# Another order of the start: the first rows of w3 by columns, products of zeros in front, banks emptied by ScalarE, one turning a step

## The chip, the cores and the metric

The kernel runs on one core of a Trainium2 chip. The metric is the device time of the launch in microseconds (us); lower is better. Before the change it is 537.89 us, the median of three runs from 537.82 to 539.18.

## The reference

Attention over a local window and a few global positions, with a bias that grows with distance, and then a feed-forward layer with a gate:

```python
# batch 4, heads 8, sequence 768, head size 64; n_global 8, n_local 96
scores = scale * np.matmul(q, k.transpose(0, 1, 3, 2))
keep = is_global | is_local                 # local: 0 <= rel < n_local
dist = np.where(is_global & ~is_local, float(n_local), np.abs(rel))
scores = np.where(keep, scores - slopes * dist, -1e9)
a = softmax(scores)                         # rows, with 1e-9 added to the sum
x = np.matmul(a, v)                         # as (3072 tokens, 512)
# feed-forward: w1, w2 (512, 1024), w3 (1024, 1024), w_out (1024, 512)
out = ((x @ w1) * (x @ w2)) @ w3 @ w_out
```

The weights arrive as 64-bit floats, two 32-bit words to a number. `n_global` and `n_local` arrive as 64-bit integers.

## The kernel before

As `w3 @ w_out` doesn't depend on the tokens, the kernel folds the two into one matrix of 1024 x 512 (eight row blocks f of 128 rows) at the start. A fold of one row block is eight products in full fp32 over the column blocks k (`F.f.k`, line 171, two records each in the trace), one PSUM bank to a block. The product is then split in a high part (`ph`, ScalarE, L174, rounds to fp32r) and a low part (`pl`, VectorE, L177). w1 and w2 are split in the same way (`wh`, L161, and `wl`, L165), one pair of 128 columns (W0 to W7) at a time. Every product with the weights is then three products in fp32r: high by high, low by high, high by low (L196 to L198 with w1 and w2, called `U`, and L224 to L226 with the folded matrix, called `Z`).

The 64-bit words are put into 32 bits by three integer operations on VectorE, `A`, `B` and `C` (L150, L152, L154). Pieces are called by kind: `o0` to `o3` are one row block of w_out each (512 KB in DRAM), `O2` and `O3` two each; `t10` is the first half of w3's row block 1 (512 KB) and `t11` the second, `T4` a whole one (1 MB). They are fetched (`d.`, L124, all on SP's queue) into eight half slots, each free again when its piece's C is done. The converted blocks of w3 lie in a pool of three buffers (tag `ag`), which later holds the gate products.

Attention runs in 24 steps s of 128 queries, for all heads: `S` scores on TensorE (L505), `R` the bias, maxima and copy on VectorE (L514, for q in 0 to 3, two operations each), `E` exponentials on ScalarE (L521), `s` the sums, `c` the scaling (L536, ScalarE in the first five steps, VectorE after), `X` the turning of the probabilities by 32 x 32 blocks on VectorE (L547, twice a step, once for each of two heads), and every second step `V`, the product with the values (L560), which leaves 256 tokens of x in PSUM; `h` and `l` split them (L583, L588). Two such pairs make a unit of 512 tokens for the feed-forward: `U.f.n.half` (n is w1 or w2), `a` the gate's copy, `g` the product (L206), `gh` and `gl` its split (L211, L216), `Z.t.j` the second product and `ot` the store.

The first unit and the first eight steps are issued by a list written out in the kernel (`ORDER`), and TensorE, VectorE, ScalarE and SP keep that order, each for itself: an instruction doesn't start before the one ahead of it on its engine, whatever is ready. GpSimd is not in the fixed order. In the list `d` is a fetch; `nt` the sizes and `bias` the tables of the bias. After the list, five more units follow, with VectorE and SP in an order that the framework finds. `fits` checks at the end whether the sizes allow the banded form; if not, `dense` does the attention again.

The bias tables (L433 to L467) need `nf`, the sizes as floats in all 128 partitions (a DMA with 128 descriptors, `nt`, and a cast, L451), `it` and `gi` (iotas on GpSimd), `qf` (the query's number in its block, GpSimd), `pr` zeroed (L446). VectorE does L451 to L458 in front of its first A.

Of the kernel before, what the change touches and what calls it, by code (L numbers as in the profile page):

```python
# [75 lines left out]
class FeedForward:  # L76

    def __init__(self, ctx, tc, w12, w3t, w_out, out):  # L80
# [610 lines left out]
```

## Time and profile before

| | |
|---|---|
| median of three runs | 537.89 us |
| the profiled execution | 539.4 us, of which the span from the first to the last instruction is 537.5 us |
| busy in the span | TensorE products 517.5, weight loads 398.2, VectorE 267.6, ScalarE 193.2, GpSimd 4.1 us |
| DMA | 53.73 MB, 100 GB/s over the span |

An engine's rows in a timeline give the start, the duration, the instruction's source line, its tile and the tiles it reads, and in brackets the time in which the engine stood idle in front of it, with what ended that. PE is TensorE's products, PEld its weight loads, DVE VectorE, ACT ScalarE, POOL GpSimd, SP the queue from which the DMAs are issued. Products overlap in the pipeline, so the pace of a stretch is read from the distance of starts and not from durations.

### The profile page before, as it was taken

How to read it: one execution, taken by the hardware profiler on the slowest of the kernel's cores; microseconds unless marked ns; L12 is line 12 of the kernel's file. 1: busy time of each engine (PE TensorE's matmuls, PEld its weight loads, DVE VectorE, ACT ScalarE, POOL GpSimd, SP SyncE). 2: the span in 40 equal slices, each digit the busy share in tenths (PEclk: the TensorE clock that was granted, in tenths of full speed). 3: DMA queues.
4: the chain of work that ended last, by engine and by line, in shares of the span. 5: the costliest groups of instructions: out<-in, count | busy, mean ns of one | idle time of the engine just before them, and what ended most of it. 6: DMA issues, size and time to landing. Idle time of an engine off the chain costs nothing.

```text
span 537.5 us, 12743 instructions
## 1 busy us (share of the span) xinstructions
PE 517.5 (96%) x5504; PEld 398.2 (74%) x5504; DVE 267.6 (50%) x714; ACT 193.2 (36%) x589; POOL 4.1 (1%) x26
## 2 busy tenths in 40 slices
PE   1999999999999999999999999999999999999995
PEld 0445457888788878888888888888888788888884
DVE  6899989994545445226455245354155363022200
ACT  5244655452523334143344144243144242222210
POOL 2000000000000000000000000000000000000000
PEclk9999999999999999999999999999999999999998
DMA  8998455600531121141022221112221101100011
GB/s 279 413 368 283 134 201 197 247 22 2 194 109 61 45 91 51 57 139 57 25 92 76 97 63 57 46 56 84 102 66 55 63 1 39 41 0 1 0 41 44
DMA packets 13985, 53.73 MB, mean 100 GB/s; under 512 B 1504, under 2 KB 3552, under 8 KB 12000
## 3 DMA queue, kind: packets, MB, share of 16 engines
q1 hardware_dynamic: 13920, 52.83, 27.7%
q8 instruction: 45, 0.74, 0.6%
q14 instruction: 20, 0.16, 0.1%
HBM read 46.53 MB, written 6.29 MB: 98 GB/s over the span
## 4 chain that ended last, share of the span: by engine, by line
PE 89%; DVE 8%; issue 1%; POOL 1%; ACT 0%; DVEq 0%; POOLq 0%
PE m L196 17%; PE m L197 16%; PE m L198 16%; PE o L224 9%; PE o L225 8%; PE o L226 8%; PE sc L560 5%; PE w L171 5%; PE sc L505 4%; DVE t L152 1%; DVE t L154 1%; DVE pr L514 1%; DVE t L150 1%; DVE wo L152 1%; DVE wo L154 0%
## 5 line engine op out<-in xcount | busy, mean ns | idle before, releaser
L196 PE MATMUL m<-xh,w12h 128*128 128x512 f32 x384 | 151.6, 395 | 0.0
L197 PE MATMUL m<-xl,w12h 128*128 128x512 f32 x384 | 149.6, 390 | 0.0
L198 PE MATMUL m<-xh,w12l 128*128 128x512 f32 x384 | 149.5, 389 | 0.0
L521 ACT ACTIVATE pr<-pr,mx 128x136 f32<-128x136 f32 (+2 forms) x192 | 74.5, 390 | 44.7 <-DVE mx L514 44.7
L196 PEld LDWEIGHTS m<-xh,w12h 128*128 128x128 f32 x384 | 72.1, 188 | 17.7 <-issue 2.7
L198 PEld LDWEIGHTS m<-xh,w12l 128*128 128x128 f32 x384 | 72.1, 188 | 15.3
L197 PEld LDWEIGHTS m<-xl,w12h 128*128 128x128 f32 x384 | 72.1, 188 | 14.3
L224 PE MATMUL o<-wh,gh 128*128 128x512 f32 x192 | 76.2, 397 | 0.0
L225 PE MATMUL o<-wl,gh 128*128 128x512 f32 x192 | 74.9, 390 | 0.0
L226 PE MATMUL o<-wh,gl 128*128 128x512 f32 x192 | 74.7, 389 | 0.0
L171 PE MATMUL w<-wo,t 128*128 128x512 f32 x128 | 61.4, 630 | 11.0 <-DVE t L154 10.9
L211 ACT ACTIVATE gh<-ag 128x512 fp32r<-128x512 f32 x48 | 30.3, 631 | 108.5 <-DVE ag L206 108.3
L206 DVE TENSOR_TENSOR ag<-m,ag 128x512 f32<-128x512 f32 x48 | 33.0, 688 | 71.6 <-PE m L198 56.3
L171 PEld LDWEIGHTS w<-wo,t 128*128 128x128 f32 x128 | 24.5, 199 | 43.1 <-issue 24.9
L588 DVE TENSOR_TENSOR xl<-sc,xh 128x1024 fp32r<-128x1024 f32 x12 | 14.7, 1224 | 65.3 <-ACT xh L583 65.3
L514 DVE CUSTOM_DVE_ANT_0 pr<-sc,biasw 128x136 f32<-128x136 f32 x160 | 36.9, 295 | 17.2 <-PE sc L505 17.2
L216 DVE TENSOR_TENSOR gl<-ag,gh 128x512 fp32r<-128x512 f32 x48 | 32.8, 684 | 23.7 <-ACT gh L211 23.7
L224 PEld LDWEIGHTS o<-wh,gh 128*128 128x128 f32 x192 | 36.0, 188 | 8.7 <-issue 1.3
L226 PEld LDWEIGHTS o<-wh,gl 128*128 128x128 f32 x192 | 36.1, 188 | 7.8
L225 PEld LDWEIGHTS o<-wl,gh 128*128 128x128 f32 x192 | 36.1, 188 | 7.0
L203 ACT ACTIVATE ag<-m 128x512 f32<-128x512 f32 x48 | 28.7, 597 | 31.6 <-PE m L198 29.5
L232 ACT ACTIVATE ot<-o 128x512 f32<-128x512 f32 x24 | 14.3, 598 | 68.3 <-PE o L226 68.3
(77 smaller groups left out, 373.5 us busy)
## 6 DMA issues: line engine op xcount, KB each, us to landing
qr<-qk SPq DMA_DIRECT2D x20, 720.0 KB, 4.3
vr<-vx SPq DMA_DIRECT2D x8, 768.0 KB, 4.4
out_dram<-ot SPq DMA_DIRECT2D x24, 256.0 KB, 2.0
raws<-w SPq DMA_DIRECT2D x3, 1024.0 KB, 6.9
more_raws<-w SPq DMA_DIRECT2D x3, 1024.0 KB, 7.6
vr<-vx SPq DMA_DIRECT2D x4, 576.0 KB, 4.3
qr<-qk SPq DMA_DIRECT2D x4, 528.0 KB, 6.6
stage<-w3t SPq DMA_DIRECT2D x4, 512.0 KB, 9.1
```

The costliest lines, as they stand in the source:

```text
L171: self.nc.tensor.matmul(self.prod[f], lhsT=self.t3[f][:, k * P:(k + 1) * P].bitcast(F32), rhs=self.wo[:, k].bitcast(F32), start=k == 0, st ...
L196: self.nc.tensor.matmul(ps, lhsT=mh, rhs=xh[:, i], start=i == 0, stop=False)
L197: self.nc.tensor.matmul(ps, lhsT=mh, rhs=xl[:, i], start=False, stop=False)
L198: self.nc.tensor.matmul(ps, lhsT=ml, rhs=xh[:, i], start=False, stop=i == NCC - 1)
L206: self.nc.vector.tensor_tensor(out=self.g[f], in0=self.ps[f, 1], in1=self.a[f], op=ALU.mult)
L211: self.nc.scalar.activation(self.gh[:, f], self.g[f], AF.Copy)
L216: self.nc.vector.tensor_tensor(out=self.gl[:, f], in0=self.g[f], in1=self.gh[:, f].bitcast(F32), op=ALU.subtract)
L224: self.nc.tensor.matmul(ps, lhsT=self.gh[:, f, ts], rhs=ff.wh[:, f], start=f == 0, stop=False)
L225: self.nc.tensor.matmul(ps, lhsT=self.gh[:, f, ts], rhs=ff.wl[:, f], start=False, stop=False)
L226: self.nc.tensor.matmul(ps, lhsT=self.gl[:, f, ts], rhs=ff.wh[:, f], start=False, stop=f == NFC - 1)
L514: nc.vector.tensor_tensor_reduce(out=pr[:, q, u, GLB + w0:GLB + w1], in0=sc[scored(u, q, w0, w1)], in1=bias, scale=-SCALE, scalar=3.0e38, ...
L521: nc.scalar.activation(x, x, AF.Exp, bias=mx[:, q, u:u + 1], scale=-1.0, accum_out=sm[:, q, u:u + 1])
```

## The change

The new order `ORDER` begins with the first four row blocks of w3 side by side, column block by column block, in place of one row block after the other; row blocks 4 to 7 follow as whole ones. Their memory layout changes with it (`w3k`). New pieces: `h0` and `h1` are column block 0 of row blocks 0 and 1, and 2 and 3 (256 KB each); `k1` to `k3` one column block of all four (512 KB); `K2` and `K3` two column blocks of all four (1 MB; column blocks 4 and 5, 6 and 7). A new step `pe` on ScalarE copies a fold's bank to SBUF; `ph` and `pl` read that copy. The sizes come by one descriptor on ScalarE's queue, are cast in one partition and spread by a product with ones (`nb`); 24 small products of zeros stand in front of `nb` and 60 behind it. The iotas are made per 32 partitions with the query's number in them, the two operations on `gd` go to GpSimd, the identity matrix is made in `dense` alone, and a small exponential is run on ScalarE at the start. `X` turns both heads in one instruction, and the moving operand of `V` becomes a strided view.

```diff
+NFH = NFC // 2
+WARM = (24,60)
 ORDER = """
-nt d.o0 d.t10 d.o1 bias d.t20 A.o0 B.o0 d.o2 C.o0 A.t10 d.T4 B.t10 C.t10 A.o1 F.1.0 B.o1 A.t20 B.t20 d.q0 C.t20 A.o2 F.2.0 d.o3 C.o1 B.o2 F.1.1 d.O2
-C.o2 F.2.1 A.T4 B.T4 F.2.2 S.0 C.T4 d.q1 F.1.2 R.0.0 R.0.1 E.0.0 A.o3 d.t21 F.4.0 E.0.1 B.o3 F.4.1 C.o3 d.t11 A.O2 F.1.3 R.0.2 F.2.3 R.0.3 d.O3 E.0.2
...
+nt bias d.o0 d.h0 d.o1 d.h1 A.o0 d.k1 B.o0 C.o0 d.k2 A.h0 B.h0 C.h0 d.o2 A.o1 F.0.0 B.o1 F.1.0 A.h1 d.o3 C.o1 B.h1 A.k1 d.k3 C.h1 B.k1 F.2.0 A.k2 C.k1
+d.K2 F.3.0 B.k2 F.0.1 A.o2 B.o2 F.1.1 C.k2 F.2.1 C.o2 d.O2 A.k3 F.3.1 A.o3 B.k3 F.0.2 B.o3 F.1.2 C.k3 d.q0 A.K2 F.2.2 C.o3 F.3.2 d.O3 B.K2 F.0.3 A.O2
+F.1.3 C.K2 F.2.3 d.K3 B.O2 S.0 C.O2 F.3.3 d.q1 R.0.0 F.0.4 R.0.1 E.0.0 A.O3 F.0.5 E.0.1 B.O3 d.T5 F.1.4 R.0.2 F.2.4 R.0.3 E.0.2 F.3.4 A.K3 E.0.3 d.T7
+B.K3 F.1.5 F.2.5 C.K3 S.1 s.0 d.W0 C.O3 c.0 F.3.5 A.T5 F.0.6 B.T5 d.q2 F.0.7 X.0 F.1.6 pe.0 ph.0 F.2.6 d.v0 R.1.0 R.1.1 F.1.7 E.1.0 R.1.2 d.q3 E.1.1
+F.2.7 R.1.3 C.T5 E.1.2 F.3.6 E.1.3 d.T4 F.3.7 A.W0 pe.1 F.5.0 s.1 B.W0 c.1 F.5.1 A.T7 d.T6 F.5.2 B.T7 F.5.3 pe.3 F.5.4 X.1 ph.3 ph.1 F.5.5 pe.2 pl.3
+V.0 ph.2 pl.0 C.W0 pl.1 wh.0 A.T4 F.5.6 h.0 C.T7 F.5.7 l.0 F.7.0 pe.5 ph.5 B.T4 F.7.1 S.2 C.T4 A.T6 F.7.2 d.q4 R.2.0 R.2.1 F.4.0 E.2.0 R.2.2 F.7.3
...
+F.6.0 B.W2 E.3.3 F.4.6 s.3 pl.7 c.3 F.4.7 C.W2 F.6.1 A.W1 F.6.2 wh.2 X.3 F.6.3 F.6.4 pe.4 wl.2 ph.4 V.1 pl.4
...
 """
...
-        self.nc.tensor.matmul(self.prod[f], lhsT=self.t3[f][:, k * P:(k + 1) * P].bitcast(F32), rhs=self.wo[:, k].bitcast(F32), start=k == 0, stop=k == NFC - 1)
+        block = self.kt[k // 2][:, (k % 2 * NFH + f) * P:][:, :P] if f < NFH else self.t3[f][:, k * P:(k + 1) * P]
+        self.nc.tensor.matmul(self.prod[f], lhsT=block.bitcast(F32), rhs=self.wo[:, k].bitcast(F32), start=k == 0, stop=k == NFC - 1)
+
+    def fold_out(self, f):
+        i = self.places.pop(0)
+        self.raw[f] = i, self.wp.tile([P, DO], F32, tag=f"wl{i}", name=f"raw_{f}")
+        self.nc.scalar.activation(self.raw[f][1], self.prod[f], AF.Copy)
 
     def fold_high(self, f):
-        self.nc.scalar.activation(self.wh[:, f], self.prod[f], AF.Copy)
+        self.nc.scalar.activation(self.wh[:, f], self.raw[f][1], AF.Copy)
 
     def fold_low(self, f):
-        self.nc.vector.tensor_tensor(out=self.wl[:, f], in0=self.prod[f], in1=self.wh[:, f].bitcast(F32), op=ALU.subtract)
+        i, raw = self.raw[f]
+        self.wl[f] = self.wp.tile([P, DO], F32R, tag=f"wl{self.free.pop()}", name=f"wl_{f}")
+        self.nc.vector.tensor_tensor(out=self.wl[f], in0=raw, in1=self.wh[:, f].bitcast(F32), op=ALU.subtract)
+        self.free.append(i)
...
+    one = pr[0:1, 0, 0, :P]
+    def warm(i):
+        if not warmth:
+            x = at.tile([P, P], BF16, tag="pt", name="warm")
+            nc.vector.memset(x, 0.0)
+            warmth.extend((x, ff.ps.tile([P, 96], F32, tag="m", name="warmed")))
+        x, y = warmth
+        for _ in range(WARM[i]):
+            nc.tensor.matmul(y, lhsT=x[:, :P], rhs=x[:, :96], start=True, stop=True)
...
-        nc.gpsimd.iota(qi, pattern=[[1, 1]], base=0, channel_multiplier=1)
-        nc.gpsimd.iota(it[:, win], pattern=[[-1, P]], base=WIN, channel_multiplier=0)
...
+        for hp in range(NP):
+            x = it[hp * R:(hp + 1) * R]
+            nc.gpsimd.iota(x[:, win], pattern=[[-1, P]], base=WIN, channel_multiplier=1)
...
+        nc.vector.tensor_copy(out=n1, in_=nt)
+        nb = ff.ps.tile([P, 4], F32, tag="m", name="nb")
+        nc.tensor.matmul(nb, lhsT=one, rhs=n1, start=True, stop=True)
+        warm(1)
         nc.gpsimd.memset(pr, 0.0)
-        nc.gpsimd.tensor_copy(out=qf, in_=qi)
...
-        nc.vector.tensor_scalar(out=dist, in0=it, scalar1=qf, scalar2=None, op0=ALU.add)
-        nc.vector.tensor_scalar(out=gd, in0=gi, scalar1=ng, scalar2=FAR, op0=ALU.is_ge, op1=ALU.mult)
+        nc.vector.tensor_copy(out=dist, in_=it)
         nc.vector.tensor_scalar(out=out, in0=dist, scalar1=0.0, scalar2=None, op0=ALU.is_lt)
-        nc.vector.tensor_scalar(out=gd, in0=gd, scalar1=nl, scalar2=None, op0=ALU.max)
+        nc.vector.tensor_copy(out=nf, in_=nb)
+        nc.gpsimd.tensor_scalar(out=gd, in0=gi, scalar1=ng, scalar2=FAR, op0=ALU.is_ge, op1=ALU.mult)
+        nc.gpsimd.tensor_scalar(out=gd, in0=gd, scalar1=nl, scalar2=None, op0=ALU.max)
...
-        x = pr[:, :, u, GLB - half * GLB:GLB - half * GLB + PF]
-        nc.vector.transpose(strided(pts[d][:, u, half * NR * PF:], [PF, NR], [P, NR + 1], [1, R]), x.rearrange("p q (k c) -> p q k c", c=R))
+        x = pr.rearrange("p q u w -> p (q u) w")[:, :, GLB - half * GLB:GLB - half * GLB + PF]
+        nc.vector.transpose(strided(pts[d][:, half * 2 * NR * PF:], [PF, 2 * NR], [P, NR + 1], [1, R]), x.rearrange("p n (k c) -> p n k c", c=R))
...
-                    nc.tensor.matmul(sc[cols, hp, q0:q1], lhsT=v[rows, i, cols], rhs=pt[rows, u, i * P + q0:i * P + q1], start=i == i0, stop=i == NV - 1, skip_group_check=True)
+                    turned = strided(pt[rows, i * P + u * PF + n0 * (2 * PF - P):], [2 * PF - P, n1 - n0], [1, R])
+                    nc.tensor.matmul(sc[cols, hp, n0 * R:n1 * R], lhsT=v[rows, i, cols], rhs=turned, start=i == i0, stop=i == NV - 1, skip_group_check=True)
...
     def sizes():
-        nc.sync.dma_start(out=nt, in_=ns.bitcast(I32).partition_broadcast(P))
+        nc.scalar.dma_start(out=nt, in_=ns.bitcast(I32).partition_broadcast(1))
+        nc.vector.memset(one, 1.0)
+        nc.scalar.activation(pr[0:1, 1, 0, :4], one[:, :4], AF.Exp)
+        warm(0)
```

## Rows read from the trace of the kernel before

**Rows 1.** The page: busy time of each engine, and the chain that ended last.
```profile
PE 517.5 (96%) x5504; PEld 398.2 (74%) x5504; DVE 267.6 (50%) x714; ACT 193.2 (36%) x589; POOL 4.1 (1%) x26
...
PE 89%; DVE 8%; issue 1%; POOL 1%; ACT 0%; DVEq 0%; POOLq 0%
```
**Rows 2.** Windows: length, busy time (count) of each engine, clock, DMA share, GB/s.
```profile
10.13:19.11 8.98, 8.20 (x20) 2.94 (x25) 7.98 (x12) 3.53 (x10) 0.25 (x2) 1.00 1.03 414
19.11:83.00 63.89, 63.27 (x776) 30.90 (x775) 59.59 (x135) 31.87 (x109) 0.00 (x0) 1.00 0.74 272
...
531.30:537.50 6.20, 0.00 (x0) 0.00 (x0) 0.00 (x0) 0.60 (x1) 0.00 (x0) 0.66 0.15 50
```
**Rows 3.** Timeline of PE: start, us, line, what, count, idle before and its releaser.
```profile
10.13 2.08 PE L171 MATMUL w<-wo,t 128*128 128x512 f32 x2 [10.13 <-DVE t L154]
12.98 6.13 PE L171 MATMUL w<-wo,t 128*128 128x512 f32 x8 [0.78 <-DVE t L154]
...
61.21 1.20 PE L505 MATMUL sc<-qr 64*32 64x136 f32 x64 [0.50 <-DVE mx L514]
...
84.38 0.39 PE L196 MATMUL m<-xh,w12h 128*128 128x512 f32 x1
...
85.06 0.39 PE L196 MATMUL m<-xh,w12h 128*128 128x512 f32 x1
```
**Rows 4.** Timeline of the weight loads, from 9 to 83 us.
```profile
14.85 0.34 PEld L171 LDWEIGHTS w<-wo,t 128*128 128x128 f32 x1 [0.52 <-issue]
...
20.93 0.19 PEld L171 LDWEIGHTS w<-wo,t 128*128 128x128 f32 x1 [0.24 <-issue]
...
22.79 0.30 PEld L171 LDWEIGHTS w<-wo,t 128*128 128x128 f32 x2 [0.81 <-DVE wo L154]
...
38.63 0.30 PEld L171 LDWEIGHTS w<-wo,t 128*128 128x128 f32 x2 [0.70 <-DVE t L154]
```
**Rows 5.** Timeline of all engines in the first 9 us.
```profile
1.19 0.42 SPq L124 DMA_DIRECT2D stage<-w_out  x1
...
2.60 1.22 POOL L446 MEMSET pr<- 128x1344 f32 x1
...
4.07 0.17 DVE L451 CAST nf<-nt 128x4 f32<-128x4 int32 x1 [4.07 <-DMA nt<-ns]
...
4.84 0.31 DVE L452 TENSOR_SCALAR dist<-it,qf 128x168 f32<-128x168 int32 x1 [0.60 <-POOL qf L450]
...
6.41 0.42 DVE L150 TENSOR_SCALAR wo<-stage 128x512 int32<-128x512 int32 x1
...
8.20 0.42 DVE L150 TENSOR_SCALAR t<-stage 128x512 int32<-128x512 int32 x1
```
**Rows 6.** Timeline of DVE, from 22 to 80 us.
```profile
28.88 1.29 DVE L154 SCALAR_TENSOR_TENSOR t<-stage,t 128x512 int32<-128x512 int32 x2
...
64.95 1.22 DVE L152 SCALAR_TENSOR_TENSOR t<-stage,t 128x1024 int32<-128x1024 int32 x1
66.08 1.56 DVE L547 STREAM_TRANSPOSE pt<-pr 128x640 f32<-128x640 f32 x2
```
**Rows 7.** DMA issues: count, KB each, us to landing; the last over the span.
```profile
stage<-w_out SPq DMA_DIRECT2D x1, 512.0 KB, 4.4
nt<-ns SPq DMA_DIRECT2D x1, 2.0 KB, 3.3
...
out_dram<-ot SPq DMA_DIRECT2D x24, 256.0 KB, 2.0
```
**Rows 8.** Groups by line and form: count, busy us, mean ns, idle before.
```profile
L514 DVE CUSTOM_DVE_ANT_0 pr<-sc,biasw 128x136 f32<-128x136 f32 x160 | 36.9, 295 | 17.2 <-PE sc L505 17.2
L216 DVE TENSOR_TENSOR gl<-ag,gh 128x512 fp32r<-128x512 f32 x48 | 32.8, 684 | 23.7 <-ACT gh L211 23.7
L177 DVE TENSOR_TENSOR wl<-w,wh 128x512 fp32r<-128x512 f32 x8 | 5.4, 682 | 0.0
L174 ACT ACTIVATE wh<-w 128x512 fp32r<-128x512 f32 x8 | 4.7, 592 | 9.6 <-PE w L171 9.6
```

More of the change, by code (lines that the diff above doesn't have):

```diff
@@ L76, with __init__ @@
 class FeedForward:
-    def __init__(self, ctx, tc, w12, w3t, w_out, out):
+    def __init__(self, ctx, tc, w12, w3k, w3t, w_out, out):
         self.nc = tc.nc
-        self.w12, self.w3t, self.w_out, self.out = w12, w3t, w_out, out
+        self.w12, self.w3k, self.w3t, self.w_out, self.out = w12, w3k, w3t, w_out, out
         self.wp = wp = ctx.enter_context(tc.tile_pool(name="wp", bufs=1))
@@ L86, in __init__ @@
         self.w = [wp.tile([P, NFC, 2, NCC, P], F32R, name=f"w12{x}") for x in "hl"]
-        self.wh, self.wl = (wp.tile([P, NFC, DO], F32R, name=n) for n in ("wh", "wl"))
+        self.wh, self.wl = wp.tile([P, NFC, DO], F32R, name="wh"), [None] * NFC
+        self.places, self.free, self.raw = list(range(NFC)), [NFC], {}
         self.wo = self.mp.tile([P, NFC, DO], I32, tag="gh", bufs=1, name="wo")
@@ L117, in fetch @@
             src = self.w_out[:, at[0] * n * DO:(at[0] + 1) * n * DO]
+        elif kind in "hkK":
+            n = len(hs)
+            src = self.w3k[:, at[0] * PC // 2:(at[0] + 1) * PC // 2] if kind == "h" else self.w3k[:, at[0] * n * PC:(at[0] + 1) * n * PC]
         else:
@@ L138, in convert @@
                 dst = self.wo[:, 2 * at[0]:2 * at[0] + 2].rearrange("p k m -> p (k m)")
+            elif kind in "hkK":
+                j = {"h": 0, "k": at[0] // 2, "K": at[0]}[kind]
+                if j not in self.kt:
+                    self.kt[j] = self.mp.tile([P, 2 * PC], I32, tag="ag", bufs=3, name=f"kt_{j}")
+                dst = self.kt[j]
+                if kind == "h":
+                    dst = dst[:, at[0] * PC // 2:(at[0] + 1) * PC // 2]
+                elif kind == "k":
+                    dst = dst[:, at[0] % 2 * PC:(at[0] % 2 + 1) * PC]
             else:
@@ L257, in attention_moe, with dense @@
 @with_exitstack
-def attention_moe(ctx: ExitStack, tc: tile.TileContext, qk, vx, w12, w3t, w_out, ns, out):
+def attention_moe(ctx: ExitStack, tc: tile.TileContext, qk, vx, w12, w3k, w3t, w_out, ns, out):
     nc = tc.nc
     cp = ctx.enter_context(tc.tile_pool(name="const", bufs=1))
-    ident = cp.tile([P, P], F32, name="ident")
-    make_identity(nc, ident)
-    nt = cp.tile([P, 4], I32, name="nt")
+    nt = cp.tile([1, 4], I32, name="nt")
+    n1 = cp.tile([1, 4], F32, name="n1")
     nf = cp.tile([P, 4], F32, name="nf")
-    ff = FeedForward(ctx, tc, w12, w3t, w_out, out)
+    ff = FeedForward(ctx, tc, w12, w3k, w3t, w_out, out)
     oki = cp.tile([P, 1], I32, name="oki")
-    banded(tc, ff, ns, nt, nf, oki, ident, qk, vx)
+    banded(tc, ff, ns, nt, n1, nf, oki, qk, vx)
     ok = nc.values_load(oki[0:1, 0:1])
     with tc.If(ok == 0):
-        dense(tc, ff, nf, ident, qk, vx)
+        dense(tc, ff, nf, qk, vx)
 @with_exitstack
-def dense(ctx, tc, ff, nf, ident, qk, vx):
+def dense(ctx, tc, ff, nf, qk, vx):
     nc = tc.nc
@@ L280, in dense @@
     with tc.tile_pool(name="dm", bufs=1) as dm, tc.tile_pool(name="dw", bufs=1) as dw, tc.tile_pool(name="dp", bufs=1, space=PSUM) as dp:
+        ident = dm.tile([P, P], F32, name="ident")
+        make_identity(nc, ident)
         nv = dm.tile([P, 2], F32, name="nv")
@@ L431, in biases @@
         gi = bp.tile([P, NR * GLB], I32, name="gi")
-        qi = bp.tile([P, 1], I32, name="qi")
-        qf = bp.tile([P, 1], F32, name="qf")
         sl = bp.tile([P, 2], F32, name="sl")
```

66 lines of the change are left out of this document (30 added, 36 removed).

## The prediction

> **What bounds the kernel now.** The page's busy shares come first [rows 1]: the TensorE queue is busy for 517.5 of 537.5 us, every other engine for half or less, and the chain that ended last is 89% PE and 8% DVE. So the reader asks for the 20 us in which PE did nothing, and for busy time that was not at full pace. The timeline of PE [rows 3] has its first instruction at 10.13, and the windows [rows 2] the rest: from 10.13 to 19.11 PE is busy for 8.20 of 8.98 us; from 19.11 to 83 some 0.6 us are idle while DVE is busy for 59.59 of 63.89 us; behind the last product, at 531.3, 6.2 us go to the last store and to the end. What lies between is PE's own work, with little idle time.
>
> The start decides. A fold product (F) has two records. In the rows of the weight loads [rows 4] a load's duration and the idle time before it give the pace: 0.19 + 0.24 = 0.43 us at 20.93, so a fold costs 0.857 us; 0.34 + 0.52 = 0.86 at 14.85: half pace, the lower of the clock's two levels (1.2 and not 2.4 GHz), although the clock column of the windows says 1.00 there. Before that PE had done nothing until 10.13 and had waited 0.78 us again. Five folds that are 4.29 us at full pace took 2.08 + 6.13 = 8.21 us [rows 3].
>
> A ledger of lost time up to the first second product (Z.0.0, after V.2, at 130.84; it is the same work in both kernels): start 10.13; half pace 8.21 - 4.29 = 3.92; the wait after the first fold, 0.78; four later waits for DVE, read as the excess of a load's idle time over the usual 0.24, from 0.57 at 22.79 to 0.46 at 38.63 and 2.3 in all [rows 4], and 0.50 for S.3 at 61.21 [rows 3]. That is 17.6 us.
>
> What ends these waits is DVE putting the 64-bit weights into 32 bits (A, B, C): their rows name it [rows 3, 4]. The DMAs are not far behind it: o0 is issued at 1.19 and lands 4.4 later, at 5.6, for an A at 6.41 [rows 5, 7].
>
> **The change part by part.** I follow the new order down the queues: an instruction begins when the one ahead of it on its engine and its inputs are done, with durations of these rows [rows 3 to 8].
>
> *Sizes and biases.* DVE's chain from 4.07 (nf) to 6.41 (first A) [rows 5] takes another path: the sizes land as one descriptor, issued by ACT, n1 is cast, PE multiplies it out to 128 partitions (nb), DVE takes nf; POOL zeroes pr (1.22 us) only when nb's product has read its ones there, then makes gd with two operations; then DVE's minimum and the first A. What goes from the front of this is the wait for qf on POOL (0.60) and two DVE operations. The DMA lands 3.3 us after issue with 128 descriptors, and a 256 KB store in 2.0 [rows 7]; I take 2.6 between these, so with the same issue (4.07 - 3.3 = 0.75) 3.35. Cast 0.17; nb is two loads at the low level (2 x 0.34 [rows 4]) and a few columns, 0.7 in all, so 4.25; zeroing 1.22, 5.45; two small POOL operations at 0.2 to 0.4 (DVE's cast 0.17, its longer operation 0.31), 6.05; DVE's minimum 0.2: the first A at 6.3 instead of 6.41. With the ends of the landing, and a slow nb, it is 5.7 to 7.2. Each 0.1 here moves everything behind by 0.1. Nine more iotas on POOL, in front of the zeroing that starts at 2.60 [rows 5], lie beside the DMA of the sizes: nothing, or some tenths if they outlast it. The activation table is loaded earlier; the bias tables behind it are first read by R.0, sixteen folds later: nothing.
>
> *First pieces.* Before the first fold stood o0 and t10, 1.78 us each (A at 6.41 to A at 8.20 [rows 5]). Now o0 and h0, half as wide: 1.0 (0.9 if it halved, 1.78 if width didn't matter). First fold at 6.3 + 1.78 + 1.0 + 0.06 = 9.15, and two folds are ready instead of one. Their data: o0 leaves SP some 0.4 us earlier, and h0 (256 KB) can take until 8.1, when DVE wants it.
>
> *Columns.* A column k needs its row of w_out and 512 numbers of w3: 2 x 1.55 us on DVE when the parts of two pieces alternate (A 0.35; B and C 0.60, as the two C of 28.88 take 1.29 with their overlap of 0.08 [rows 6]) and yields four folds, 3.43 us. From K2 on, pairs of columns: 2 x (0.6 + 1.14 + 1.14) = 5.8 for 6.86 us of folds (1.13 from 64.95 to 66.08 [rows 6]). So PE, once two columns are in, is the slower one, and DVE's lead has to pay for R.0 (1.4), R.1 (8 x 36.9/160 = 1.85 [rows 8]), two s (0.3 each) and X.0. One place isn't covered: behind F.0.0 and F.1.0, which end at 10.86, DVE does o1, h1 and a part of k1 (2.8 us) until 12.0: PE waits 1.2. Up to C.O3, which frees columns 6 and 7, DVE has 9.3 for o1 to o3 and k1 to k3, 1.0 for h1, 11.6 for O2, O3, K2 and K3, 1.7 for R.0 and s.0 and about 1 for parts that follow their own piece's part: 33.7 us; PE comes there at 12.0 + 22 x 0.857 + S.0 and S.1, 2.3 = 33.2. So the two run side by side to some tenths. Walking on, I find waits of 0.3 at F.0.4 (O2), 0.25 at F.7.0 (a bank) and 0.5 at V.1 (X.3): 2.3 in all. DMA: a megabyte at 414 GB/s [rows 2] takes 2.55 us and DVE 2.9 to 3.1 for it, so they stay ahead, by two or three microseconds at q0 and O2.
>
> *Small products of zeros.* 24 in front of nb, 60 behind it. No row has such products. Below: 96 of 512 columns at the pace of the U products, 0.68 / 3 = 0.227 us apart from 84.38 to 85.06 [rows 3], is 0.043 us, or 0.085 at the lower level; above: a full-width weight load that nothing hides, 0.34 + 0.085 = 0.42. I take 0.09 falling to 0.05, as the U products, each with a load of its own, are spaced by their columns alone. From 4.25 the 60 end between 7.3 and 9.4, in front of or at the first fold. At the upper end, 4.25 + 25 = 29.4. The folds should then run at 0.857 from the start: the 3.92 us go. If they don't, little is lost, as PE then only uses up its waits: with half pace until 13 us the walk ends at the same time, with half pace until 17 us 1.9 us later.
> The Trainium skill ("TensorE: Matmul & The Clock Gate", Part 1) says that the array's clock is halved by default and sustained activity releases it; the trace agrees, 0.86 and then 0.43 us between loads [rows 4]. The Trainium skill (the same page, Part 2, "Back-to-back issue gap") has 81 ns for sustained pairs of a load and a 128-column product; by that, as an estimate, the 60 would end at 9.1 at full pace and at 14.0 at half, which speaks against the change: a first fold up to 4.8 us late.
>
> *Banks.* pe puts eight copies of 0.59 us (4.7/8, as L174 [rows 8]) on ACT, which is busy for half of the stretch [rows 2]; banks come free without waiting for pl on DVE. pl now reads SBUF: L216 does so in 0.684 us, L177 from PSUM in 0.682 [rows 8], so nothing. With PE in front of DVE by only some tenths at F.7.0 and V.1, what ACT delays is worth up to 1.5 us.
>
> *Turning.* One instruction for two that take 1.56 us together [rows 6]: some 0.05 less on DVE, 24 times, nearly all beside PE. The products of V now read runs of 32 numbers, as many as before: nothing, at worst a few tenths a V, 2 us over the twelve.
>
> *Sum.* Lost in front of Z.0.0: 9.15 + 2.3 + 0.2 for four restarts = 11.65. The same walk of the old order finds 16.6 (start 10.2, half pace 3.2, waits 1.1, 0.5, 0.2 and 1.0, restarts 0.4) where the rows have 17.6, so I add 1.0: 12.65, against 17.6. That is 4.95 us less. Behind Z.0.0 the work of PE and the 6.2 us at the end are the same: nothing. S.7 comes later in the order but has about 2 us to spare for its data. The span becomes 532.6, the profiled execution 539.4 - 4.9 = 534.5; the median of the runs shown is 1.5 below the profiled execution, so 537.9 - 4.9 = **533.0 us**.
>
> **The rivals.**
> 1. *The products of zeros outlast the data* (slower). They stand in PE's queue in front of the first fold; each microsecond past 9.15 costs one, less PE's 2.3 us of waits, which it uses up. From 0.2 us each (end at 16.3) the gain is gone; at 0.34 (a weight load at the low level [rows 4]) they end at 24.7 and the time is 533.0 + 15.5 - 2.3 = 546. For: each has its own load. Against: U's loads are hidden [rows 3].
> 2. *Late sizes.* POOL's zeroing sits behind nb and in front of gd. First A at 7.2: 533.9.
> 3. *The clock stays low or falls back* in PE's 1.2 us wait, until 17 us: 534.9.
> 4. *The DMAs don't keep up.* h pieces have rows of half the length. At 3.1 us a MB, PE waits 0.9, 1.0, 0.5, 0.5 and 1.4 us at F.0.3, S.0, F.0.4, V.0 and F.7.0: 537.2, no change. Against: 414 GB/s from 10.13 to 19.11 [rows 2].
> 5. *ACT or DVE late at F.7.0, V.1 or U.5.0.0* (the last has 0.7 us): 2 to 3 us, 535.5.
>
> **How the numbers follow.** Forecast (531 to 534.5) 0.52; rival 1 0.09; 2 0.10; 3 0.08; 4 0.09; 5 0.12. 0.3% (1.6 us) is what a measurement of this kernel can tell from no change. Faster: forecast, 2, 3 and 5, 0.82 less 0.01 for a bad case of 5: 0.81; same: 4 and a bit of 1 and 5, 0.11; slower: 0.08. The range is 531.0 (all of PE's waits gone, or the first A at 5.7) to 537.0, which leaves out rival 1 and half of rival 4.
>
> **What would show it.** PE's first fold at 8.6 to 10 us, its loads 0.43 apart at once; one wait of about 1.2 us behind two folds; U.0.0.0 at 76 to 77 instead of near 83 (six products ahead of 84.38 [rows 3]) and the end of V.2 near 126; the stretch behind equal in length. A first fold past 11, or spacings of 0.85 past 17 us, or DVE waiting for DMAs before 30 us, would make the prediction wrong.

## The result and the profile after

The changed kernel takes 532.92 us, median of four runs from 532.52 to 533.43; the kernel before took 538.53 on the same chip (537.82 to 540.07). The ratio is 0.9893 [0.9876, 0.9910], faster by 1.1%. The prediction was 533.0 in 531.0 to 537.0. The profiled execution took 532.95 with a span of 531.2, against 539.4 and 537.5.

Busy times and the chain that ended last, from the page of the changed kernel, against [rows 1]. PE's share of the chain rises from 89% to 97%, DVE's falls from 8% to 1%: what DVE still sets is the start and a few short waits. ACT has 5.4 us more, the copies of the banks among them, and is still at 37%.

```profile
PE 520.4 (98%) x5590; PEld 403.8 (76%) x5590; DVE 265.6 (50%) x691; ACT 198.6 (37%) x598; POOL 5.0 (1%) x30
...
PE 97%; DVE 1%; POOL 0%; issue 0%; ACT 0%; POOLq 0%
```

Windows of the changed kernel, columns as in [rows 2]: up to the first fold, up to 19.11, up to the first product of U. Between 9.16 and 19.11 PE is idle for 0.98 us, from 19.11 to 76.00 for 0.12; the short waits inside that window are hidden in the busy times of matmuls whose ends are modelled, so they are read from the loads below.

```profile
0.00:9.16 9.16, 6.84 (x86) 6.53 (x86) 4.86 (x16) 5.68 (x13) 4.85 (x29) 1.00 0.80 284
9.16:19.11 9.95, 8.97 (x21) 3.86 (x22) 9.88 (x21) 1.76 (x6) 0.12 (x1) 1.00 0.93 340
19.11:76.00 56.89, 56.77 (x700) 28.00 (x699) 55.45 (x121) 35.35 (x115) 0.00 (x0) 1.00 0.67 262
```

The timeline of all engines up to the first fold, against [rows 5] and the first of [rows 3]. The sizes are in SBUF by 1.93, the spread product (nb) stands behind the 24 products of zeros until 3.16, POOL zeroes pr from 3.90 to 5.12 and only then makes gd; DVE waits 1.27 us for that. The 60 products of zeros end at 7.96, 1.20 us ahead of the first fold, which DVE's conversion of h0 releases.

```profile
0.74 0.51 ACTq L639 DMA_DIRECT2D nt<-ns  x1
1.12 2.10 PE L464 MATMUL warmed<-warm 128*128 128x96 bf16 x24 [1.12 <-DVE warm L460]
1.93 0.16 DVE L484 CAST n<-nt 1x4 f32<-1x4 int32 x1 [0.86 <-DMA nt<-ns]
3.16 0.59 PE L486 MATMUL nb<-n,pr 1*128 1x4 f32 x2
3.67 4.29 PE L464 MATMUL warmed<-warm 128*128 128x96 bf16 x60
3.90 1.22 POOL L488 MEMSET pr<- 128x1344 f32 x1 [0.21 <-PE nb L486]
5.60 0.37 POOL L493 TENSOR_SCALAR gd<-gd,nf 128x32 f32<-128x32 f32 x1
6.01 0.19 DVE L496 TENSOR_TENSOR dist<-dist,gd 128x32 f32<-128x32 f32 x1 [1.27 <-POOL gd L493]
6.12 0.42 DVE L165 TENSOR_SCALAR wo<-stage 128x512 int32<-128x512 int32 x1
9.16 1.98 PE L187 MATMUL w<-wo,kt 128*128 128x512 f32 x4 [1.20 <-DVE kt L169]
```

The timeline of PE, against [rows 3]: one wait of 0.98 behind F.0.0 and F.1.0, then folds without a gap in this view, U.0.0.0 at 76.05.

```profile
12.12 11.40 PE L187 MATMUL w<-wo,kt 128*128 128x512 f32 x26 [0.98 <-DVE kt L169]
...
76.05 0.80 PE L220 MATMUL m<-xh,w12h 128*128 128x512 f32 x1
```

The weight loads, against [rows 4]: 0.19 + 0.24 us between folds from the first pair on. Three waits show as a longer idle time: for the piece O2 of w_out at F.0.4 (0.74 - 0.24 = 0.50), for O3 at F.0.6 (0.21), and at F.7.0 (0.68).

```profile
9.70 0.19 PEld L187 LDWEIGHTS w<-wo,kt 128*128 128x128 f32 x1 [0.24 <-issue]
...
25.40 0.30 PEld L187 LDWEIGHTS w<-wo,kt 128*128 128x128 f32 x2 [0.74 <-DVE wo L169]
...
33.48 0.40 PEld L187 LDWEIGHTS w<-wo,kt 128*128 128x128 f32 x2 [0.45 <-DVE wo L169]
...
50.15 0.30 PEld L187 LDWEIGHTS w<-wo,t 128*128 128x128 f32 x2 [0.92 <-ACT xh L622]
```

That last row names ACT's split of x (h.0), but the split ends at 49.70, 0.45 us earlier. The timeline of ACT has a copy that empties a bank at 50.09; it isn't what F.7.0 waits for either, as it ends at 50.69. The timeline of DVE has the end that fits: the last operation (C) of w3's row block 7, which F.7.0 reads, ends at 50.03. In every other trace of this order with the copies, too, the load of F.7.0 stands 0.11 or 0.12 us behind the end of this operation. So this is a wait for DVE's conversion.

```profile
48.69 1.01 ACT L622 ACTIVATE xh<-sc 128x1024 fp32r<-128x1024 f32 x1
50.09 0.60 ACT L192 ACTIVATE raw<-w 128x512 f32<-128x512 f32 x1 [0.39 <-PE w L187]
```
```profile
48.82 1.21 DVE L169 SCALAR_TENSOR_TENSOR t<-raws,t 128x1024 int32<-128x1024 int32 x1
```

A load stands ahead of its product, so its idle time says more than PE loses. The timeline of PE gives the loss by starts: 14 products without a wait take 6.21 us (53.19 to 59.40), and each one more or fewer counts 0.43. From 24.36 to 31.61 are 16, so F.0.4 loses 0.18; from 48.07 to 52.06 are 8, so F.7.0 loses 0.35; F.0.6 loses 0.01 (30 products from 32.73 to 45.81), and the wait behind F.1.0 costs 1.22 (30 from 9.16 to 23.45).

```profile
24.36 7.32 PE L187 MATMUL w<-wo,kt 128*128 128x512 f32 x16
31.61 1.20 PE L543 MATMUL sc<-qr 64*32 64x136 f32 x64
...
48.07 4.06 PE L187 MATMUL w<-wo,t 128*128 128x512 f32 x8
52.06 1.20 PE L543 MATMUL sc<-qr 64*32 64x136 f32 x64
53.19 6.28 PE L187 MATMUL w<-wo,t 128*128 128x512 f32 x14
59.40 1.20 PE L543 MATMUL sc<-qr 64*32 64x136 f32 x64
```

Groups by form, against [rows 8] and the pair of turnings in [rows 6]: pl from SBUF as long as from PSUM, the copy 0.58 us, one turning of both heads 1.51 us.

```profile
L585 DVE STREAM_TRANSPOSE pt<-pr 128x1280 f32<-128x1280 f32 x24 | 36.1, 1506 | 0.7 <-ACT pr L574 0.3
...
L200 DVE TENSOR_TENSOR wl<-raw,wh 128x512 fp32r<-128x512 f32 x8 | 5.4, 676 | 0.7 <-ACT wh L195 0.7
...
L192 ACT ACTIVATE raw<-w 128x512 f32<-128x512 f32 x8 | 4.7, 583 | 2.1 <-PE w L187 2.1
```

Two marks split the gain. The first product behind V.2 starts at 130.77 before and at 125.55 after, in the same view (the 130.84 of the ledger is V.2's end by the chain): 5.22 us. In two repeats of the changed kernel (E2 and E13 below) the first mark is at 125.28 and 125.27, so it is good to 0.3 us. The last product of all starts at 530.91 before and at 524.53 after: 6.38. So 1.16 us come from the stretch that was to be equal. PE has few idle places there. The timeline of PE before has two, both inside a V (V.4 and V.10, counting from V.0; the expectations below call them V.5 and V.11):

```profile
186.36 2.61 PE L560 MATMUL sc<-pt,vr 32*64 32x32 f32 x168
189.95 0.43 PE L560 MATMUL sc<-pt,vr 32*64 32x64 f32 x24 [0.98 <-issue]
...
420.18 0.46 PE L560 MATMUL sc<-pt,vr 32*64 32x64 f32 x31 [1.30 <-issue]
```

The timeline of PE after has one, inside V.8 (V.9 in the expectations):

```profile
334.03 2.77 PE L599 MATMUL sc<-pt,vr 32*64 32x32 f32 x187
337.85 0.31 PE L599 MATMUL sc<-pt,vr 32*64 32x32 f32 x5 [1.05 <-issue]
```

0.98 + 1.30 - 1.05 = 1.23. "issue" says that no data and no buffer was waited for. The table of DMA queues of the kernel before, around V.4 (187 to 191.5), has the instruction queue at work: two fetches of 16 KB, one at 187.62 and one at 191.02, 3.4 us apart. Around V.8 of the changed kernel they are at 335.53 and 338.90.

```profile
q8 instruction: 2, 0.03, 2.9%
```

A V of 192 records is a load and a product each, 384 instructions in 2.8 us, 0.007 us for one; a product of U takes 0.23 us, with a load beside it. The changed kernel's 11,180 products and loads come with 46 of these 16 KB transfers (the queue's line on the page, q8), 243 to one; I take 256, an estimate. So PE goes through a block inside V faster than blocks came here (1.9 us against 3.4). Which V meets the end of its store would then hang on where in a block it begins, and that on how many instructions stand in front of it. That was the theory to test.

### The profile page after: what moved, and what is told of

Its sections match the earlier page's. It is cut to its first block, busy times and chain, and to the rows that moved or that the text cites. A ratio compares the mean times of both kernels' runs of the same rounds, so it can differ in the third digit from the quotient of the medians.

```text
span 531.2 us, 12910 instructions
## 1 busy us (share of the span) xinstructions
PE 520.4 (98%) x5590; PEld 403.8 (76%) x5590; DVE 265.6 (50%) x691; ACT 198.6 (37%) x598; POOL 5.0 (1%) x30
## 4 chain that ended last, share of the span: by engine, by line
PE 97%; DVE 1%; POOL 0%; issue 0%; ACT 0%; POOLq 0%
PE m L220 17%; PE m L221 16%; PE m L222 16%; PE w L187 10%; PE o L248 9%; PE o L249 8%; PE o L250 8%; PE sc L599 6%; PE sc L543 5%; PE warmed L464 0%; DVE wo L167 0%; DVE wo L169 0%; POOL pr L488 0%; DVE kt L167 0%; DVE kt L169 0%
## 5 line engine op out<-in xcount | busy, mean ns | idle before, releaser
L585 DVE STREAM_TRANSPOSE pt<-pr 128x1280 f32<-128x1280 f32 x24 | 36.1, 1506 | 0.7 <-ACT pr L574 0.3
L559 ACT ACTIVATION_READ_ACCUMULATOR pr<-pr,mx 128x1 f32 x192 | 36.0, 188 | 0.0
```

What stands on the lines that cost most here:

```text
L559: nc.scalar.activation(x, x, AF.Exp, bias=mx[:, q, u:u + 1], scale=-1.0, accum_out=sm[:, q, u:u + 1])
L585: nc.vector.transpose(strided(pts[d][:, half * 2 * NR * PF:], [PF, 2 * NR], [P, NR + 1], [1, R]), x.rearrange("p n (k c) -> p n k c", c=R))
```

## The experiments

Medians in us, with the ratio to the kernel before as it ran on the same chip, and the idle time "issue" of PE inside the V, from the profiled run. A single idle place is V.8's. The kernel before had medians of 539.22 beside E1 to E4, 538.44 beside E5 to E9 and 539.12 beside E10 to E13.

```
kernel                          median  ratio [95%]               idle inside V
changed (first result)          532.92  0.9893 [0.9876, 0.9910]   1.05
E1 no zeros                     534.39  0.9914 [0.9898, 0.9930]   2.41
E2 zeroing behind gd (repeat)   533.12  0.9887 [0.9871, 0.9903]   1.45
E3 old order, 120 zeros         540.16  1.0027 [1.0011, 1.0044]   3.31
E4 no copies of banks           539.80  1.0020 [1.0002, 1.0038]   0.99
E5 70 zeros more                536.97  0.9976 [0.9962, 0.9989]   5.17
E6 two turnings a step          532.49  0.9888 [0.9870, 0.9906]   1.02
E9 gd on DVE                    531.98  0.9880 [0.9863, 0.9897]   1.15
E7 gd on DVE, h1 first          532.00  0.9881 [0.9863, 0.9898]   1.07
E10 six zeros fewer             532.69  0.9881 [0.9866, 0.9897]   0, but 1.01 behind V.8
E11 start sooner                532.56  0.9875 [0.9859, 0.9890]   0, but 1.14 behind V.8
E12 old order, 80 zeros         536.22  0.9943 [0.9929, 0.9957]   0, but 0.42 behind V.8
E13 changed, again              532.76  0.9884 [0.9869, 0.9899]   0.98
```

**E1: no products of zeros.**

```
-WARM = (24,60)
+WARM = (0, 0)
```

> The changed kernel without its 84 products of zeros. Theory 'supply' (the gain is what DVE has ready when; the prediction's): the first fold stays at 9.16 us but runs at half pace for the 7.5 us that the kernel before needed from its first fold to full pace; the 3.7 us that this costs are taken in part from PE's waits (1.0 behind the second fold, 0.5 and 0.7 later), so the time is 1.3 to 1.9 us above the changed kernel's, about 534.5. Rival 'clock' (the gain is mainly the folds at half pace): 3.9 us above, 536.8.

Measured: 1.5 us slower than the changed kernel, as the theory of supply expected. The weight loads of E1: from the first fold at 9.01 a load and its gap take 0.86 us, the lower of the two levels, and from 14.04 on 0.43 to 0.46.

```profile
10.03 0.34 PEld L187 LDWEIGHTS w<-wo,kt 128*128 128x128 f32 x1 [0.52 <-issue]
...
14.04 0.19 PEld L187 LDWEIGHTS w<-wo,kt 128*128 128x128 f32 x1 [0.27 <-issue]
```

S.0 begins at 24.44, 0.99 later than in the changed kernel, and V.0 at 47.08, 1.27 later. The 0.3 between the two are not the zeros' doing: the timeline of DVE has a wait for O2's DMA, which comes late in this run, and F.0.4 waits for O2.

```profile
22.34 0.69 DVE L165 TENSOR_SCALAR wo<-raws 128x1024 int32<-128x1024 int32 x1 [1.28 <-DMA raws<-w_out]
```

The seven products up to 14.04 take 5.0 us where 3.0 would do (0.43 each), and half of these 2 us come out of waits for DVE that follow anyway. So the zeros are worth about 1 us through the clock here, not the 3.9 that the half-pace folds of the old order had lost. Behind V.2 the profiled run can't stand for the median: with 536.64 it is the longest of five (from 533.87). Its V idle for 2.41 us, 1.36 more than in the changed kernel, though no product of zeros is near. And behind V.10, which has 1.53 of these, the granted clock falls to the lower level (0.51 in the windows, columns as in [rows 2]). Products of U stand 0.43 us apart until 419.93, not 0.23, which costs another 1.5 us.

```profile
418.00:420.00 2.00, 2.00 (x6) 1.54 (x6) 1.30 (x2) 0.39 (x1) 0.00 (x0) 0.51 0.82 332
```

Neither theory had that.

**E2: POOL's zeroing of pr behind gd.**

```
-        nc.gpsimd.memset(pr, 0.0)
         ...
+        nc.gpsimd.memset(pr, 0.0)          (behind the two operations on gd)
```

> The changed kernel with POOL's zeroing of pr moved behind its two operations on gd, one line. The chain in front of the first A then has no 1.22 us of zeroing in it: gd done near 4.75, minimum near 4.8, first A at 4.95 instead of 6.12, first fold near 8.0 instead of 9.16. Theory 'supply': everything behind moves by as much, 1.1 us less than the changed kernel, about 531.8. Rival 'DMA': the pieces land too late for an earlier DVE (o0 has landed at 4.55, h0 at 5.1, o1 at 6.4), waits behind the first folds grow and the time stays, 532.9.

This failed as a test. The order on POOL is not written out, and the zeroing still ran first (3.89), the first A at 6.11, the first fold at 9.17. It is a repeat of the changed kernel, with its time.

**E3: the old order with products of zeros in front.** 120 of them, 96 columns each, in the kernel before.

```
+        nc.vector.memset(x, 0.0)
+        for _ in range(120):
+            nc.tensor.matmul(y, lhsT=x[:, :P], rhs=x[:, :96], start=True, stop=True)
```

> The kernel before with 120 products of zeros in front of its first fold (they end near 9.7, the first fold is due at 10.13), and nothing else. Theory 'supply': the five folds at half pace (3.9 us) become waits for DVE in part, F.2.0 waits 2.0 instead of 0.8 us and others 0.5 more; 1.8 us less than before, 0.9967 of it. Rival 'clock': 3.9 us less, 0.9928.

The first fold is at 10.11 and at full pace at once, and the next pair waits 1.73 us for DVE. The first product behind V.2 starts at 128.92, 1.85 earlier than before, as expected, but the total got none of it. The timeline of PE has three idle V where the kernel before has two, 3.31 us against 2.28; one of them:

```profile
185.71 1.48 PE L560 MATMUL sc<-pt,vr 32*64 32x160 f32 x86
188.26 0.35 PE L560 MATMUL sc<-pt,vr 32*64 32x32 f32 x16 [1.07 <-issue]
```

In the profiled run (538.82, among the shorter of twelve from 538.11 to 543.01) the last product stands 0.44 us earlier than before. An idle place costs somewhat more than its idle time: a V of 192 records takes 2.75 us up to the next product, and the three take 4.02, 4.36 and 3.95, together 4.08 more; the two of the kernel before take 2.65 more. 1.85 less 1.43 is 0.42. The median, 0.9 above that of before, has another 1.3 us that this trace doesn't show. They go with the granted clock: its mean is 0.997 and 0.999 in the runs of 538.11 and 538.82, 0.989 to 0.994 in the ten others (539.43 and more), and 0.995 to 0.999 in all runs of the kernel before beside them. E1's trace shows such a fall behind an idle V; that it is the same here is likely, and no trace of one of the ten was kept. The zeros alone do not carry the change; why more V are idle this run leaves open, and E12 takes it up.

**E4: without the copies of the banks.** wh is made from PSUM and pl reads PSUM, as before; the order is the changed one, its pe steps empty.

```
-        self.nc.scalar.activation(self.raw[f][1], self.prod[f], AF.Copy)
-        self.nc.scalar.activation(self.wh[:, f], self.raw[f][1], AF.Copy)
+        self.nc.scalar.activation(self.wh[:, f], self.prod[f], AF.Copy)
         ...
+        self.nc.vector.tensor_tensor(out=self.wl[f], in0=self.prod[f], in1=self.wh[:, f].bitcast(F32), op=ALU.subtract)
```

> The changed kernel without the copies of the banks on ScalarE: high and low parts read PSUM again, the order stays. The bank of F.5.0 is then free only behind pl.0, which stands in DVE's order behind X.1 and T7, near 46 us, where PE wants it near 40. Theory 'the copies are what this order stands on': PE waits some 6 us there, 538 to 540. Rival 'banks are free in time anyway': no difference, 532.9.

As expected: PE waits 5.11 us for a bank that pl, late in DVE's order, still reads, and the gain is gone. Behind the wait the loads are at the lower level again until 49.32: five products take 3.46 us, 1.3 more than at full pace. The weight loads of E4 there:

```profile
45.86 0.50 PEld L187 LDWEIGHTS w<-wo,t 128*128 128x128 f32 x2 [5.94 <-DVE wl L197]
46.88 0.34 PEld L187 LDWEIGHTS w<-wo,t 128*128 128x128 f32 x1 [0.52 <-issue]
...
49.32 0.19 PEld L187 LDWEIGHTS w<-wo,t 128*128 128x128 f32 x1 [0.40 <-issue]
```

So this order stands on the copies: row blocks 0 to 3 hold four banks at once, and pl may come late only because a copy keeps the numbers. An order made for it without copies might do better; that was not tried.

**E5: 70 products of zeros more.**

```
-WARM = (24,60)
+WARM = (24, 130)
```

> The changed kernel with 130 instead of 60 products of zeros behind nb. At the last pace of the 60 (18 in 0.88 us, 0.049 each) they end near 11.4 us, so the first fold starts 2.25 us later than 9.16. Theory 'supply': PE's waits of 0.98 (behind the second fold), 0.5, 0.2 and 0.68 us take that up, V.2 ends 0 to 0.5 us later than at 125.6. Rival 'the start is PE's': V.2 ends 2.2 us later. Second theory, on the idle times of about 1 us inside V ('issue', in this trace with two 16 KB instruction fetches 3.4 us apart around each): 140 PE instructions more move the fetches against the work, so such idle times stand in other V (not at V.9, 337.85, where the changed kernel has its one); against that, they belong to V.5, V.9 and V.11 whatever stands in front.

The first fold moves from 9.16 to 10.86, and yet V.0 begins only 0.26 later (46.07): PE uses up its waits, which cost 1.22 and 0.18 by the starts of its products. V.1 begins 0.10 earlier, at 70.92. That is the supply theory. But V.2 ends 3.1 us later and not 0 to 0.5, and the kernel is 4 us slower: four V are idle (V.1, V.2, V.5 and V.11), for 1.42, 1.38, 1.36 and 1.01 us. They take 5.99 us more than 2.75 each, V.8 of the changed kernel 1.30; 4.69 - 0.10 = 4.59, and the last products stand 4.58 apart (529.11 and 524.53). Two of the four, in the timeline of PE:

```profile
75.02 0.33 PE L599 MATMUL sc<-pt,vr 32*64 32x32 f32 x11 [1.42 <-issue]
...
128.36 0.36 PE L599 MATMUL sc<-pt,vr 32*64 32x64 f32 x17 [1.38 <-issue]
```

V.8 has none now, as the second theory expected. 70 products are 140 instructions; nothing else behind the first folds is different, and idle places 65 to 450 us later appeared and vanished.

**E6: two turnings a step**, with the same layout of pt.

```
+        for u in range(2):
+            x = pr[:, :, u, GLB - half * GLB:GLB - half * GLB + PF]
+            nc.vector.transpose(strided(...), x.rearrange("p q (k c) -> p q k c", c=R))
```

> The changed kernel with two turnings a step of half the size in place of one, same layout. Theory 'one turning is worth nothing here': 0.05 to 0.1 us more on DVE a step, hidden but for the first three; time within 0.3 us of 532.9. Rival: DVE is the bound of the start and pays for each, 4 x 0.1 plus waits at V.0 and V.1, 0.5 to 1 us more.

532.49, the changed kernel's time: turning both heads in one instruction is worth nothing that these runs can tell.

**E9 and E7: gd on DVE; and with it h1 in front of o1.**

```
-        nc.gpsimd.tensor_scalar(out=gd, in0=gi, ...)
-        nc.gpsimd.tensor_scalar(out=gd, in0=gd, ...)
+        nc.vector.tensor_scalar(out=gd, in0=gi, ...)
+        nc.vector.tensor_scalar(out=gd, in0=gd, ...)

E7 also:
-... A.o1 F.0.0 B.o1 F.1.0 A.h1 d.o3 C.o1 B.h1 A.k1 d.k3 C.h1 B.k1 F.2.0 ...
+... A.h1 F.0.0 B.h1 F.1.0 C.h1 d.o3 A.o1 A.k1 d.k3 B.o1 F.2.0 B.k1 C.o1 ...
```

> The changed kernel with the two operations on gd on DVE again, where they need not wait for POOL's zeroing (in e2 POOL kept the zeroing in front all the same, so that run was the changed kernel once more). DVE stood idle there for 1.27 us. First A near 5.2 instead of 6.12 (o0 has landed at 4.55), first fold near 8.25. Theory 'supply': everything up to V.2 moves by 0.9 us, 532.0. Rival 'DMA': pieces land too late (k1 9.1, k2 10, o2 10.8, o3 12.4), the waits behind the first folds grow by as much, no change.

> As e9, and h1 is converted right behind h0, ahead of o1, so that four folds are ready before column 1 is wanted. The wait behind F.1.0 (0.98 us) goes; PE then waits at F.0.1 for k1 and o1, some 0.5 us. Theory 'supply': 0.5 us less than e9, 531.5 (or 531 if the column wait is absorbed). Rival: the later wait takes all of it, as e9.

In E9 the first A comes at 5.81, 0.31 sooner and not the 0.9 that leaving POOL's chain should give. The timeline of all engines in E9 shows where the rest went: an operation on 128x32 takes 1.10 us beside POOL's zeroing and ends with it; in E11, where POOL doesn't zero, the same takes 0.24. The next one, L493, ends with the zeroing too.

```profile
3.89 1.22 POOL L488 MEMSET pr<- 128x1344 f32 x1 [0.21 <-PE nb L486]
4.05 1.10 DVE L492 TENSOR_SCALAR gd<-gi,nf 128x32 f32<-128x32 int32 x1
4.20 0.95 DVE L493 SCALAR_TENSOR_TENSOR out<-dist,nf,out 128x168 f32<-128x168 f32 x1
5.18 0.24 DVE L494 TENSOR_SCALAR gd<-gd,nf 128x32 f32<-128x32 f32 x1
```

The first fold is at 8.86 in both. In the profiled run of E9, the longest of its four, a DMA was 0.89 us late for K2, so the first product behind V.2 stands at 126.17; E7 has it at 125.08, 0.2 to 0.5 before the three traces of the changed kernel. E7's wait moves from F.2.0 to F.0.1, the next column, as its rival had it. E9's median meets its expected 532.0 with a third of the expected move, so not by that sum. Both medians are 0.5 below E6, which ran beside them, and 0.8 below E13 on the same chip, but the intervals of the ratios overlap: a gain that is likely and not shown.

**E10 and E11: six zeros fewer; everything sooner.** E10 takes 12 instructions out in front of V.8, to move it off its place. E11 adds to E7 that DVE zeroes pr at 1.29, before the sizes are there, and has 10 + 68 products of zeros.

```
E10:
-WARM = (24,60)
+WARM = (24, 54)
E11, beside the lines of E7:
-WARM = (24,60)
+WARM = (10, 68)
-        nc.gpsimd.memset(pr, 0.0)
+        nc.vector.memset(pr, 0.0)          (ahead of the sizes)
```

> The changed kernel with 54 instead of 60 products of zeros behind nb: 12 PE instructions fewer (a load and a product each). Theory 'fetches': in all traces so far a V of 192 records stands idle for 1 to 1.5 us when its first instruction is number 48 to 116 past a multiple of 256 (16 KB) of PE's stream, and does not at 4 to 36 or 128 to 244; V.9 stands at 48 in the changed kernel and comes to 36, and V.7 from 144 to 132; so no V waits any more, 1.0 to 1.3 us less than the changed kernel on the same chip, first fold at 9.16 as before. Rival 'idle times by chance': same time within 0.3 us, and an idle time of about 1 us somewhere in a V.

> As e7 (gd on DVE, h1 right behind h0), and pr zeroed by DVE in its idle time near 1.1 us in place of POOL, the ones in other memory, 10 zeros in front of nb and 68 behind it (12 PE instructions fewer in all, as in e10). nb ends near 2.8, first A at 4.6 to 4.7 (o0 has landed at 4.55), first fold near 7.5, the zeros end near 7.7. Theory 'supply': 1.2 us less than e7 and 1.0 from the fetches, near 530. Rival 'DMA': o1, h1, k1, k2 land at 6.3, 7.7, 9.1 and 10.0, later than DVE then wants them; the first folds come sooner and the waits behind them grow, near 531.

E10's expectation failed. The idle place left V.8, but only for the products right behind it, and the time stayed:

```profile
334.35 2.82 PE L599 MATMUL sc<-pt,vr 32*64 32x32 f32 x192
337.10 0.50 PE L220 MATMUL m<-xh,w12h 128*128 128x512 f32 x1
338.61 0.50 PE L221 MATMUL m<-xl,w12h 128*128 128x512 f32 x1 [1.01 <-issue]
```

E11 brings the first A to 4.58, and then three things are late in turn: the zeros, which end at 8.71 by the model and let the first fold go at 8.51; the transfers, DVE waiting 0.29 and 0.30 us for K2 and O2; and, for want of O2, PE at 24.94 for 0.88. The two waits for DMAs, in the timeline of DVE:

```profile
17.88 0.69 DVE L165 TENSOR_SCALAR kt<-stage 128x1024 int32<-128x1024 int32 x1 [0.29 <-DMA stage<-w3k]
...
20.61 0.69 DVE L165 TENSOR_SCALAR wo<-raws 128x1024 int32<-128x1024 int32 x1 [0.30 <-DMA raws<-w_out]
```

Of 1.54 us at the first A 0.7 are left at the first product behind V.2 (124.84), 0.4 against the repeat E13. At the end 532.56 against 532.76 for the repeat: no difference that can be told, where 530 or, by the rival, 531 was expected.

**E12 and E13: the old order with 80 zeros of 176 columns; the changed kernel again.** E12 is E3 with 40 products, that is 80 instructions, fewer, each with more columns (80 x 176 against 120 x 96), chosen by the rule below so that no V would begin at a bad place.

```
+        for _ in range(80):
+            nc.tensor.matmul(y, lhsT=x[:, :P], rhs=x, start=True, stop=True)
```

> The kernel before with 80 products of zeros of 176 columns in front (e3 had 120 of 96), which end near 10. Theory 'fetches': all V of 192 records come to 180, 192, 4, 164, 132, 36, 4 and 164 past a multiple of 256, so none stands idle (the kernel before has two, 2.3 us; e3 three, 3.3 us or more): 2.3 us less for that and 1.85 us less by V.2 as in e3, 0.992 to 0.993 of before. Rival (zeros in front of the old order bring nothing, as e3's 1.0027 says): 0.999 to 1.003.

> The changed kernel as it is, on the same chip as e10 and e11, to compare them with: about 0.989 of before, one idle time in V.9.

0.9943 [0.9929, 0.9957] against E3's 1.0027 [1.0011, 1.0044], somewhat less gain than the 0.992 to 0.993 expected and clear of the rival. The first product behind V.2 is 2.0 us earlier than before, in E3 1.85; no V is idle inside, and 0.42 us are behind V.8. The last product stands at 526.82, 4.1 earlier than before, where E3's stands 0.44 earlier. So the same change at the start is worth 0.6% or nothing, by where instruction blocks fall, and with the falls of the clock that most runs of E3 have. E13 came out as expected.

**The rule.** I counted PE's records in the traces, two instructions each, and took for each V of 192 records the place of its first instruction modulo 256. Every V that idles inside begins at 48, 60, 76, 84, 88, 100, 104 or 116, in every kernel whose records were counted; none does that begins at 4 to 36 or at 132 to 244, and no V of 144 records. At 36 the idle time stands just behind the V in E10, E11 and E12, and there is none in E1 (V.2). The counts are complete: 5,504 products in the kernel before, and beside them the zeros and two for nb. That the place decides is shown by E5, E10 and E12, which change the count of instructions in front. That it is the fetch of the next block that is waited for rests on "issue" and on the transfers of that queue: in all 21 idle places of the fourteen traces PE goes on 1.25 to 1.51 us after the end of a 16 KB transfer. Two transfers some 3.5 us apart are not enough: the kernel before has a pair around V.8 (340.02 and 343.53), which doesn't idle. No run slowed or sped a fetch.

## Why the prediction came out right

*The start.* Predicted 4.95 us less up to Z.0.0, measured 5.22. First A 6.3 and 6.12; first fold 9.15 and 9.16. The sum was right, three of its terms were not. The sizes landed 1.2 us after issue and not 2.6, below the lower end that I gave; and nb, ready to go at 2.1, then stood behind the 24 products of zeros, which take 2.10 us together, until 3.16. I had counted those 24 at nothing: they hide behind a slow DMA, and this one was quick. From the first A to the first fold it is 3.04 and not 2.85. That these cancel to a hundredth is luck. POOL's zeroing from 3.90 then set gd, as the forecast had it.

*The zeros.* 60 in 4.29 us, 0.07 each, between the 0.05 and 0.09 taken. From start to start it is 0.080 until 7.05 and 0.043 for the last 18, the two paces that the prediction worked out below its own choice. They end 1.2 us ahead of the first fold. The Trainium skill ("TensorE: Matmul & The Clock Gate", Part 2, "Back-to-back issue gap") gives 81 ns for a pair with 128 columns and gave 9.1 to 14.0 for their end, as an estimate, from the start predicted for them, 4.25; the trace, where they start at 3.67 and have 96 columns, has 7.96 and decides.

*Half pace.* The folds run at 0.43 us between loads from the first pair on. That undoes the 3.92 us of the ledger in name, but E1 shows what it is worth in the new order: about 1 us. The walk had said nothing for half pace until 13 us and 1.9 until 17; E1 is at half pace until 14.0, so that lies between. The bulk of the start's gain is the rest of the change: E1 has it without zeros, 4.19 us at the first product behind V.2, and E3 has zeros without it, 1.85. The rest is the order by columns with its smaller first pieces, the new path of the sizes and the copies together; no run has the columns alone.

*The waits.* Read from the loads, 1.2 became 0.98, 0.3 at F.0.4 became 0.50, and there are 0.21 at F.0.6; 0.25 at F.7.0, put down to a bank, became 0.68 (0.37 in E2 and E13), and it is DVE's conversion of w3's row block 7 that is late; 0.5 at V.1 did not come. Sum 2.37 against 2.25. This reading overstates, in the ledger too: by the starts of products its four later waits cost 1.05 us and not 2.3, half pace and the wait after the first fold 4.42 and not 4.70, S.3's 0.56; with the start's 10.13 that is 16.16 us and not 17.6. The changed kernel loses 9.16 + 1.22 + 0.18 + 0.01 + 0.35 = 10.92, and the difference of 5.24 is the 5.22 that was measured. So the 1.0 that the prediction added to its walk was mostly no loss of PE's; as it stands on both sides, the forecast didn't suffer.

*Banks and turning.* The copies cost 0.58 us each, 0.59 predicted, and sit beside other work; what they are worth was not in the prediction, and E4 shows that without them this order loses all. Turning: nothing, E6.

*Behind Z.0.0.* "Nothing" was the step that failed: -1.23 us, all of it in idle time "issue" inside V, at places that the trace of before had too. I had passed over those two as PE's own. That the new order has one such place and not four, as with E5's 70 more zeros, is luck. The median moved by 5.6 us where the profiled runs moved by 6.4; the runs of before spread by 2.2 us, so the two do not differ by more than that.

*The rivals.* 1: the zeros don't outlast the data, and E5 bears out its price, the delay less PE's waits (1.70 becomes 0.26); idle V, which it did not have, made E5 slower. 2: not late. 3: the pace did not fall behind the 0.98 us wait, but it did behind the 5.11 of E4. 4: DVE waits 0.20 us for a DMA of weights before 30 us in the changed kernel, at 26.09, which by the letter was a sign of being wrong and cost nothing that shows. In single runs the DMAs are later, with the start moved forward (E9 0.89, E11 0.29 and 0.30) and without (E1 1.28, E10 0.51); E2, E5, E6, E7 and E13 have no such wait. 5: of its three places F.7.0 alone was late, by DVE and not by ACT, for 0.35 by the starts where I had 2 to 3 in all.
